# One transformer block on one core: the condition and beta fetched as one row each and spread by TensorE, one block of the modulation weights loaded and multiplied ahead of x

## The chip, the core and the metric

The kernel runs on one core of a Trainium2 chip. The metric is device time in microseconds (us) of one launch, and less is better. Three runs of the kernel before took 853.75, 854.21 and 854.20 us; their median is 854.2 us. Three abbreviations for engines come from the profile: PE is TensorE, DVE is VectorE, ACT is ScalarE; POOL is GpSimd and SP is SyncE, which issues most DMAs.

## The reference

The block takes x (2048 rows of 512), a condition row c (1x512) and weights, all in fp32. The change touches what is computed from c, from `beta` and from the first 1024 columns of `w_mod`:

```python
mod = (_silu(c) @ w_mod).reshape(c.shape[0], 6, 1, -1)
sa, ca, ga, sb, cb, gb = (mod[:, 0], mod[:, 1], mod[:, 2], mod[:, 3], mod[:, 4], mod[:, 5])
h = _layernorm(x, axis=-1) * (1 + ca) + sa
x = x + ga * _A_ref(h, A_wq, A_wk, A_wv, A_wo, A_beta)
h = _layernorm(x, axis=-1) * (1 + cb) + sb
x = x + gb * _B_ref(h, B_w_gate, B_w_up, B_w_down)
```

`_A_ref` is attention of 32 heads of width 16 over four segments of 512 rows, with a memory carried from segment to segment. `sigmoid(beta)`, one number a head, mixes memory and attention. `_B_ref` is a bilinear GLU of width 1376.

## The kernel before

The program is one long function, `tile_kernel`, that writes instructions out in order. It has three stages: a start, which ends with the projections of the first segment's first heads; attention with the rest of the projections woven in; and the GLU. PE's instructions are chained one behind the other in the order in which the code writes them (`MM`, `TP`), and `CV` and `CA` do the same for DVE and ACT in the start. So the order in the start is that of the code. DMAs issued by SP run in the order of SP's queue. Each DMA takes one of eight completion semaphores in turn (those of ACT's queue too), so an issue waits until the DMA eight places before it has landed.

All of the change lies in the start:

- ACT's queue fetches the condition as `s_c` (L628): the host has laid c out as 128 rows of 4 numbers, so 16 bytes go to each of 128 partitions. It then fetches `beta` to all 128 partitions as `be` (L669), 128 bytes each, all from the same source row.
- SP fetches x's first four tiles (`xload`, L643; 256 KB each), then the first half of the needed modulation weights (`wm0_load(0)`, L665): four blocks `wm0[k]`, 256 KB each, one for each group of 128 input rows. Behind these come `wk`'s first piece (L759), the second half (`wm0_load(1)`), `wq`'s first piece and four blocks of `wv`.
- PE runs 18 matmuls of zeros (`warm`, `wups`), each 128x512 in bf16, whose result nothing reads.
- ACT and DVE make silu(c) in `s_c` (L670 to L673): exp, plus one, reciprocal, product. GpSimd's four memsets of `kst` wait for the product.
- DVE takes the statistics of the four x tiles (`BATCH_NORM_STATS2`), ACT and DVE make 1/sd, and DVE normalises the tiles in place (`ln`, L203).
- PE computes the first half of sa and ca: `mod0(0)` (L719) multiplies four groups of 128 columns by silu(c), k = 0 to 3, with `s_c` repeated to 96 columns as the moving operand. A matmul in fp32 stands as two in the profile, so that is 32 passes. Then PE transposes the normalised x (`atp`, 16 transposes).
- For the second half, ACT scales block 0 by silu(c), DVE adds block 1 to that (`SCALAR_TENSOR_TENSOR`, L1112), and `mod0(1, (1, 2, 3))` needs 24 passes. Behind these stand the first projections `kps` and `qps`.

The call order at the start is this:

```python
lng = ln(pa, pa, xts.pop(0), 0, ca_c, sa_c, "a", ("h", 8, 2), True)
next(lng)                                        # statistics, 1/sd
mod0(0)
CA.activation(r0[1][0], r0[1][0], AF.Copy, scale=s_c[:, 0:1])
next(lng)                                        # normalise, transpose
mod0_out(0, mp0[0])
CV.scalar_tensor_tensor(r0[1][1], r0[1][1], s_c[:, 1:2], r0[1][0], op0=ALU.mult, op1=ALU.add)
mod0(1, (1, 2, 3))
```

## Time and profile before

| | |
|---|---|
| median of three runs | 854.2 us |
| the profiled execution's own time | 854.15 us |
| its span, first to last instruction | 852.4 us |
| PE busy | 835.3 us, 98% |
| DVE, ACT, POOL busy | 643.1, 499.0, 276.8 us |
| first matmul on real data begins | 8.79 us |
| first projection (`kps`) begins | 16.97 us |

Times in the views count from the span's start. A row of the timeline gives the start, the time from the first start to the last end of the merged instructions, the engine, the line, the operation with what it writes and reads, and in brackets how long the engine sat idle before it and what ended that. "SPq" and "ACTq" are the sequencers that issue DMAs; a DMA's duration there is the issue alone, and its time to landing stands in the view of DMA issues. A row of the view by windows gives for each stretch the busy time of each engine with the number of its instructions, the granted clock, the DMA engines' busy share and GB/s.

### The profile page before, as it was taken

How to read it: one execution, taken by the hardware profiler on the slowest of the kernel's cores; microseconds unless marked ns; L12 is line 12 of the kernel's file. 1: busy time of each engine (PE TensorE's matmuls, PEld its weight loads, DVE VectorE, ACT ScalarE, POOL GpSimd, SP SyncE). 2: the span in 40 equal slices, each digit the busy share in tenths (PEclk: the TensorE clock that was granted, in tenths of full speed). 3: DMA queues.
4: the chain of work that ended last, by engine and by line, in shares of the span. 5: the costliest groups of instructions: out<-in, count | busy, mean ns of one | idle time of the engine just before them, and what ended most of it. 6: DMA issues, size and time to landing. Idle time of an engine off the chain costs nothing.

```text
span 852.4 us, 14404 instructions
## 1 busy us (share of the span) xinstructions
PE 835.3 (98%) x4972; PEld 597.4 (70%) x4972; DVE 643.1 (75%) x1797; ACT 499.0 (59%) x760; POOL 276.8 (32%) x423
## 2 busy tenths in 40 slices
PE   9989999999999999999999999999999999999998
PEld 6756656666665656666665687888888778888886
DVE  7897768887778967787888359989987855447654
ACT  4758767787676876677545626344435555555330
POOL 2756627566565774675434610000000000000000
PEclk9999999999999999999999999999999999999999
DMA  9645435563545554466675466587650685335102
GB/s 271 155 152 155 121 104 141 158 179 115 143 106 166 144 165 106 122 170 213 195 216 155 145 192 230 189 287 271 253 201 28 234 271 210 121 135 184 43 8 98
DMA packets 83928, 139.57 MB, mean 164 GB/s; under 512 B 12720, under 2 KB 46768, under 8 KB 83856
## 3 DMA queue, kind: packets, MB, share of 16 engines
q1 hardware_dynamic: 83424, 138.51, 52.0%
q8 instruction: 39, 0.64, 0.3%
q14 instruction: 33, 0.27, 0.1%
q10 hardware_dynamic: 432, 0.15, 0.1%
HBM read 89.87 MB, written 48.50 MB: 162 GB/s over the span
## 4 chain that ended last, share of the span: by engine, by line
PE 61%; DVE 5%; ACT 1%; issue 0%; POOL 0%; DVEq 0%
PE acc L1358 14%; PE Xg L1289 7%; PE Xu L1289 6%; PE wops L85 5%; PE tb L85 5%; PE Yu L1289 4%; PE Yg L1289 4%; PE k L85 3%; PE q L85 3%; DVE q L39 2%; PE Zg L1289 1%; PE Zu L1289 1%; PE qps L85 1%; PE vps L85 1%; PE Xx L1289 1%; PE up L85 1%
## 5 line engine op out<-in xcount | busy, mean ns | idle before, releaser
L39 DVE CUSTOM_DVE_ANT_0 q<-q,cmask 128x384 f32<-128x384 f32 (+3 forms) x512 | 248.2, 503 | 71.1 <-PE q L85 63.5
L335 ACT ACTIVATE pt<-k 128x1024 f32<-128x1024 f32 x160 | 164.0, 1025 | 74.2 <-PE k L85 71.4
L341 POOL TENSOR_SCALAR_AFFINE_SELECT pt<-pt 128x256 f32<-128x256 f32 (+1 forms) x224 | 98.0, 452 | 137.2 <-ACT pt L335 136.9
L85 PE MATMUL q<-kst,qst 96*128 96x384 bf16 (+3 forms) x512 | 122.8, 302 | 6.5 <-DVE nm L39 5.1
L85 PE MATMUL k<-qst,kst 98*128 98x384 bf16 (+3 forms) x512 | 96.0, 299 | 1.6 <-ACT pt L335 1.3
L1366 DVE TENSOR_TENSOR xa<-xa,acc 128x512 f32<-128x512 f32 x95 | 64.9, 684 | 39.6 <-PE acc L1358 37.8
L85 PEld LDWEIGHTS <-qst 96*128 96x128 bf16 x512 | 43.9, 98 | 58.4 <-issue 43.6
L85 PE MATMUL tb<-pt,v 128*32 128x512 f32 (+3 forms) x1024 | 75.5, 436 | 0.0
L39 DVE DVE_READ_ACCUMULATOR2_ANT nm<- 128x1 f32 x512 | 71.8, 140 | 0.0
L85 PEld LDWEIGHTS <-kst 98*128 98x128 bf16 x512 | 44.4, 98 | 24.9 <-issue 8.8
L1358 PE MATMUL acc<-dH,mH 128*128 128x512 f32 (+1 forms) x152 | 60.3, 397 | 0.0
L1358 PE MATMUL acc<-dL,mH 128*128 128x512 f32 (+1 forms) x152 | 60.1, 395 | 0.0
L1358 PE MATMUL acc<-dH,mL 128*128 128x512 f32 (+1 forms) x152 | 60.0, 395 | 0.0
L85 PEld LDWEIGHTS tb<-pt,v 128*32 128x32 f32 x1024 | 28.7, 109 | 38.6 <-issue 35.7
L367 ACT ACTIVATE tsb<-tb 128x512 f32<-128x512 f32 x32 | 19.1, 596 | 31.6 <-PE tb L85 31.5
L1358 PEld LDWEIGHTS acc<-dH,mL 128*128 128x128 f32 (+1 forms) x152 | 28.5, 188 | 7.1 <-DVE mL L1309 0.3
L1358 PEld LDWEIGHTS acc<-dL,mH 128*128 128x128 f32 (+1 forms) x152 | 28.6, 188 | 7.0
L1358 PEld LDWEIGHTS acc<-dH,mH 128*128 128x128 f32 (+1 forms) x152 | 28.5, 188 | 6.8
L85 PE MATMUL kps<-ahH,wkH 128*128 128x512 f32 x64 | 29.4, 460 | 0.0
L85 PE MATMUL qps<-ahH,wqH 128*128 128x512 f32 x64 | 28.7, 448 | 0.2 <-DVE oL L39 0.2
L85 PE MATMUL vps<-wvH,ahH 128*128 128x512 f32 x64 | 28.3, 442 | 0.0
L85 PE MATMUL wops<-woH,oH 128*128 128x512 f32 x64 | 28.3, 442 | 0.0
(403 smaller groups left out, 2019.1 us busy)
## 6 DMA issues: line engine op xcount, KB each, us to landing
wm<-in_w_mod_dram SPq DMA_DIRECT2D x24, 256.0 KB, 3.9
kd<-k SPq DMA_DIRECT2D x16, 384.0 KB, 2.5
qd<-q SPq DMA_DIRECT2D x16, 384.0 KB, 3.5
kst<-kd SPq DMA_DIRECT2D x32, 192.0 KB, 3.2
qst<-qd SPq DMA_DIRECT2D x32, 192.0 KB, 3.7
x<-in_x_dram SPq DMA_DIRECT2D x16, 256.0 KB, 4.8
kst<-kd SPq DMA_DIRECT2D x32, 128.0 KB, 3.2
qst<-qd SPq DMA_DIRECT2D x32, 128.0 KB, 3.7
```

Source lines behind the costliest of these rows:

```text
L39: i = getattr(self.eng, name)(*a, **k)
L85: return pe(nc.tensor.matmul(*a, **k))
L335: ex = act.activation(pt, kp, AF.Exp, scale=0.25)
L341: sels[u, i] = nc.gpsimd.affine_select(w, w, pattern=[[0, w.shape[1]], [1, P]], compare_op=ALU.is_ge, fill=0.0, base=0, channel_multiplier=-1)
L367: act.activation(tsbs[u], tbs.pop(u), AF.Copy)
L1289: pe(nc.tensor.matmul(ps[0:n], a, b[:, k], start=first and c == 0, stop=last and c == 5, skip_group_check=True))
L1358: pe(nc.tensor.matmul(ps, a[0:m, t * P:(t + 1) * P], b[0:m], start=j == 0, stop=j == n - 1))
L1366: vec.tensor_add(xa, xa, ps)
```

## The change

The host passes c as one row. ACT's queue fetches it as one row of 512 numbers (`crow`), and beta as one row of 32 (`brow`). PE turns the condition into columns, by four matmuls of one contraction row each, and copies beta to all partitions by one more; both results stand in the second bank of `wups`. ACT and DVE read the condition there, and ACT copies beta into `be`. Of the first half of the modulation weights, block k = 0 is loaded ahead of x and multiplied ahead of the others. The 18 matmuls of zeros become nine: three at the start, two behind the spreading and four behind the product of block 0.

```diff
-    nc.scalar.dma_start(s_c, c)
+    crow = pa.tile([P, D], F32, tag="mem", name="crow", bufs=1)[0:1]
+    brow = pa.tile([P, D], F32, tag="pkr", name="brow", bufs=1)[0:1, 0:H]
+    nc.scalar.dma_start(crow, c)
+    nc.scalar.dma_start(brow, beta[None, :])
...
-    xts = {0: xload(0)}
-    NWU = 18
...
-    warm(NWU)
...
-    wm0_load(0)
+    wm0_load(0, (0,))
+    xts = {0: xload(0)}
...
+    warm(3)
+    cps = wups[:, 1, 0:KT]
+    for k in range(KT):
+        MM(cps[:, k:k + 1], crow[:, k * P:(k + 1) * P], ones[0:1, 0:1], start=k == 0, stop=k == KT - 1, skip_group_check=True)
+    bps = wups[:, 1, KT:KT + H]
+    MM(bps, ones[0:1, :], brow, start=True, stop=True, skip_group_check=True)
+    warm(2)
+    wm0_load(0, (1, 2, 3))
     r0 = [[a[:, j].rearrange("p i c -> p (i c)") for a in wm0] for j in range(2)]
-    nc.scalar.dma_start(be, beta[None, :].to_broadcast([P, H]))
-    act.activation(e1, s_c, AF.Exp, scale=-1.0)
-    CV.tensor_scalar_add(e1, e1, 1.0)
-    CV.reciprocal(e1, e1)
-    scl = CV.tensor_mul(s_c, s_c, e1)
+    act.activation(e1, cps, AF.Exp, scale=-1.0)
+    act.activation(be, bps, AF.Copy)
+    def condition():
+        CV.tensor_scalar_add(e1, e1, 1.0)
+        CV.reciprocal(e1, e1)
+        scl = CV.tensor_mul(s_c, cps, e1)
...
     lng = ln(pa, pa, xts.pop(0), 0, ca_c, sa_c, "a", ("h", 8, 2), True)
+    condition()
     next(lng)
-    mod0(0)
+    mod0(0, (0,))
+    warm(4)
+    mod0(0, (1, 2, 3))
```

In `mod0` the moving operand and the start flag are chosen by the half j and no longer by the list of blocks, which leaves the products what they were.

On PE, at the head of its queue, the program before has the 18 matmuls of zeros (two of their rows are shown), then the product of all four blocks (`m`, from `wm`), then the transposes of x:

```order
L85 LDWEIGHTS wu
L85 MATMUL wups<-wu 128x512
L85 MATMUL m_248<-s_c,wm_0_231 128x96 x4
L85 MATMUL m_248<-s_c,wm_1_232 128x96 x4
L85 MATMUL m_248<-s_c,wm_2_233 128x96 x4
L85 MATMUL m_248<-s_c,wm_3_234 128x96 x4
L88 MATMUL atp_0_318<-ident,x_0_202 128x128
```

In the changed program PE has this from the third matmul of zeros on, down to the second of the four that follow block 0:

```order
L85 MATMUL wups<-wu 128x512
L85 MATMUL wups<-ones,crow 128x1 x4
L85 MATMUL wups<-brow,ones 128x32
L85 LDWEIGHTS wu
L85 MATMUL wups<-wu 128x512
L85 LDWEIGHTS wu
L85 MATMUL wups<-wu 128x512
L85 MATMUL m_236<-s_c,wm_0_205 128x96 x4
L85 LDWEIGHTS wu
L85 MATMUL wups<-wu 128x512
L85 LDWEIGHTS wu
L85 MATMUL wups<-wu 128x512
```

So the spreading stands behind three matmuls of zeros, block 0 behind two more, and the other three blocks behind four more; from the transposes on, PE's order is the same in both programs.

SP's queue at its head, before:

```order
L643 DMA x_0_202<-in_x_dram 128x512
L643 DMA x_1_204<-in_x_dram 128x512
L643 DMA x_2_206<-in_x_dram 128x512
L643 DMA x_3_208<-in_x_dram 128x512
L665 DMA wm_0_231<-in_w_mod_dram 128x2x256
L665 DMA wm_1_232<-in_w_mod_dram 128x2x256
```

And in the changed program:

```order
L657 DMA wm_0_205<-in_w_mod_dram 128x2x256
L646 DMA x_0_210<-in_x_dram 128x512
L646 DMA x_1_212<-in_x_dram 128x512
L646 DMA x_2_214<-in_x_dram 128x512
L646 DMA x_3_216<-in_x_dram 128x512
L657 DMA wm_1_206<-in_w_mod_dram 128x2x256
```

One block of the weights has moved past the four tiles of x; what follows stands as before. DVE's order has not moved: the three steps of the condition still stand directly ahead of the first statistics of x. ACT has one instruction more, the copy of beta, behind the exp of the condition.

More of the change, by code (lines that the diff above doesn't have):

```diff
@@ L645, in xload, with wm0_load @@
         return xt
+    wm0 = []
+    for k in range(KT):
+        a = ap.tile([P, 2, 2, 256], F32, tag="pt", name=f"wm0_{k}", bufs=PT)
+        wm0.append(a)
+    def wm0_load(j, ks=range(KT)):
+        for k in ks:
+            pin(nc.sync.dma_start(wm0[k][:, j], wm[:, k, :].rearrange("p (i c) -> p i c", c=D)[:, 0:2, 256 * j:256 * j + 256]))
+    wm0_load(0, (0,))
     xts = {0: xload(0)}
-    NWU = 18
     wu = pa.tile([P, 512], BF, tag="rl", name="wu", bufs=1)
@@ L655, in warm @@
             MM(wups[:, 0], wu[:, 0:P], wu, start=True, stop=True)
-    warm(NWU)
-    wm0 = []
+    warm(3)
+    cps = wups[:, 1, 0:KT]
     for k in range(KT):
-        a = ap.tile([P, 2, 2, 256], F32, tag="pt", name=f"wm0_{k}", bufs=PT)
-        wm0.append(a)
-    def wm0_load(j):
-        for k in range(KT):
-            pin(nc.sync.dma_start(wm0[k][:, j], wm[:, k, :].rearrange("p (i c) -> p i c", c=D)[:, 0:2, 256 * j:256 * j + 256]))
-    wm0_load(0)
-    r0 = [[a[:, j].rearrange("p i c -> p (i c)") for a in wm0] for j in range(2)]
-    nc.scalar.dma_start(be, beta[None, :].to_broadcast([P, H]))
-    act.activation(e1, s_c, AF.Exp, scale=-1.0)
-    CV.tensor_scalar_add(e1, e1, 1.0)
-    CV.reciprocal(e1, e1)
-    scl = CV.tensor_mul(s_c, s_c, e1)
-    for a in kst:
-        tc.add_manual_dep(nc.gpsimd.memset(a[96:98].rearrange("p h t -> p (h t)").bitcast(F32), ONES2).ins, scl.ins.name, SYNC, reason="order")
+        MM(cps[:, k:k + 1], crow[:, k * P:(k + 1) * P], ones[0:1, 0:1], start=k == 0, stop=k == KT - 1, skip_group_check=True)
[3 more added lines that the diff above has]
+    wm0_load(0, (1, 2, 3))
+    r0 = [[a[:, j].rearrange("p i c -> p (i c)") for a in wm0] for j in range(2)]
+    act.activation(e1, cps, AF.Exp, scale=-1.0)
[4 more added lines that the diff above has]
+        scl = CV.tensor_mul(s_c, cps, e1)
+        for a in kst:
+            tc.add_manual_dep(nc.gpsimd.memset(a[96:98].rearrange("p h t -> p (h t)").bitcast(F32), ONES2).ins, scl.ins.name, SYNC, reason="order")
     def gates():
@@ L721, in mod0 @@
         for k in ks:
-            f = s_c[:, k:k + 1].to_broadcast([P, MW]) if len(ks) == KT or k > 1 else ones[:, 0:MW]
+            f = s_c[:, k:k + 1].to_broadcast([P, MW]) if j == 0 or k > 1 else ones[:, 0:MW]
             for i in range(4):
                 MM(ps[:, i], r0[j][k][:, i * P:(i + 1) * P], f,
-                   start=k == ks[0] and i == 0, stop=k == KT - 1, skip_group_check=True)
+                   start=k == j and i == 0, stop=k == KT - 1, skip_group_check=True)
     hcur = [None]
@@ L1669 @@
     vals[0] = vals[0].reshape(S, D)
-    vals[9] = vals[9].reshape(KT, P).T
+    vals[9] = vals[9].reshape(1, D)
     nc = _bacc.Bacc("TRN2", target_bir_lowering=False, num_devices=1, dynamic_dma_scratch_size=1024)
```

## Prediction

> **What bounds the kernel now.** I read the page first, then PE's waits, then the start in order of time, because the change ends at PE's instruction for the first transpose.

> ```profile
> span 852.4 us, 14404 instructions
> PE 835.3 (98%) x4972; PEld 597.4 (70%) x4972; DVE 643.1 (75%) x1797; ACT 499.0 (59%) x760; POOL 276.8 (32%) x423
> PE q L85 <- DVE nm L39: 5.1, 11, 1.0
> PE q L85 <- DMA qd<-q: 0.5, 1, 0.5
> DVE ast L39 <- DMA x<-in_x_dram: 1.0, 2, 0.5
> 17.00:38.00 21.00, 20.91 (x91) 16.38 (x91) 18.09 (x26) 17.36 (x28) 11.06 (x21) 1.00 0.77 178
> ```

> PE is busy 98% of the span. The next three rows are waits (total, times, longest): PE's greatest behind 17 us, its only one there for a DMA, and DVE's for x in the start. The last is a window: from 17 to 38 us PE is busy 20.91 of 21.00 us. PE, in program order, is the path, so the change is worth what it moves `kps`, the first projection, and the rest follows at the same distance. The start, in order of time:

> ```profile
> 0.82 1.81 SPq L643 DMA_DIRECT2D x<-in_x_dram  x4
> 1.69 6.82 PE L85 MATMUL wups<-wu 128*128 128x512 bf16 x18 [1.69 <-DVE wu L650]
> 2.67 2.38 SPq L665 DMA_DIRECT2D wm<-in_w_mod_dram  x4
> 3.70 0.20 ACT L670 ACTIVATE e<-s_c 128x4 f32<-128x4 f32 x1 [1.61 <-DMA s_c<-in_c_dram]
> 4.35 0.16 DVE L39 TENSOR_TENSOR s_c<-s_c,e 128x4 f32<-128x4 f32 x1
> 4.43 0.69 DVE L39 BATCH_NORM_STATS2 ast<-x 128x6 f32<-128x512 f32 x1
> 7.25 0.69 DVE L39 BATCH_NORM_STATS2 ast<-x 128x6 f32<-128x512 f32 x1 [0.50 <-DMA x<-in_x_dram]
> 8.07 0.66 DVE L39 BATCH_NORM_STATS2 ast<-x 128x6 f32<-128x512 f32 x1
> 8.77 0.18 DVE L39 BATCH_NORM_AGGREGATE amv<-ast 128x2 f32<-128x6 f32 x1
> 8.79 3.78 PE L85 MATMUL m<-s_c,wm 128*128 128x96 f32 x32 [0.27 <-DVE ast L39]
> 10.35 1.91 DVE L39 TENSOR_SCALAR x<-x,amv,ay 128x512 f32<-128x512 f32 x4
> 12.41 1.91 PE L88 MATMUL atp<-ident,x 128*128 128x128 f32 x16
> 12.58 0.72 ACT L39 ACTIVATE wm<-wm,s_c 128x512 f32<-128x512 f32 x1 [3.06 <-DMA wm<-in_w_mod_dram]
> 12.61 0.16 DVE L39 COPY modc<-m 128x2 f32<-128x2 f32 x1 [0.34 <-PE m L85]
> 12.68 0.15 DVE L39 TENSOR_SCALAR modc<-m 128x2 f32<-128x2 f32 x1
> 13.21 1.14 ACT L39 ACTIVATE wkH<-wrk 128x512 fp32r<-128x512 f32 x1
> 13.46 0.75 DVE L39 SCALAR_TENSOR_TENSOR wm<-wm,s_c,wm 128x512 f32<-128x512 f32 x1 [0.63 <-DMA wm<-in_w_mod_dram]
> 14.27 1.13 PE L85 MATMUL m<-ones,wm 128*128 128x96 f32 x8
> 15.24 1.95 PE L85 MATMUL m<-s_c,wm 128*128 128x96 f32 x16
> 16.97 0.48 PE L85 MATMUL kps<-ahH,wkH 128*128 128x512 f32 x1
> 26.84 1.84 POOL L765 TENSOR_TENSOR wkL<-wrk,wkH 128x512 fp32r<-128x512 f32 x1 [18.58 <-ACT wkH L39]
> ```

> From 8.79 us PE hardly rests: 32 passes to 12.41 (0.113 us each), 16 transposes, a wait of about 0.1 us for DVE's sum (done at 13.46 + 0.75 = 14.21), 24 passes to 16.97. What released the first pass was not DVE, as its bracket says, but a landing: the first `wm` issue (2.67) took 6.0 us to land, which is 8.67. These are the landing times, from the DMA views of the stretches 0.8 to 1.2 (two rows), 2.6 to 3.0, and 4.0 to 5.2 us:

> ```profile
> x<-in_x_dram SPq DMA_DIRECT2D x1, 256.0 KB, 2.7
> s_c<-in_c_dram ACTq DMA_DIRECT2D x1, 2.0 KB, 2.8
> wm<-in_w_mod_dram SPq DMA_DIRECT2D x1, 256.0 KB, 6.0
> wm<-in_w_mod_dram SPq DMA_DIRECT2D x2, 256.0 KB, 6.6
> ```

> Why does a block take 2.7 us at first and 6 later? The last two columns of the next rows are the DMA engines' busy share and GB/s; the last two rows are the queues between 3.5 and 5.5 us.

> ```profile
> 2.50:3.10 0.60, 0.60 (x3) 0.30 (x2) 0.27 (x2) 0.00 (x0) 0.00 (x0) 1.00 1.59 341
> 3.60:4.60 1.00, 1.00 (x3) 0.30 (x2) 0.59 (x4) 0.20 (x1) 0.00 (x0) 1.00 0.33 94
> 4.60:5.60 1.00, 1.00 (x4) 0.40 (x3) 0.70 (x2) 0.00 (x0) 0.96 (x2) 1.00 0.26 84
> 6.10:7.10 1.00, 1.00 (x4) 0.30 (x2) 0.62 (x2) 0.23 (x1) 1.00 (x2) 1.00 1.05 394
> q1 hardware_dynamic: 95, 0.16, 25.8%
> q10 hardware_dynamic: 103, 0.01, 3.7%
> ```

> The stream runs at 341 GB/s, falls to 94 and 84, and returns to 394. In the hole, 103 packets of q10 (ACT's queue) carry 0.01 MB: beta's 128 copies. Queue and hole coincide; that one causes the other is my inference. [...] The rows show a hole, but not its cause.

> **The change part by part.** The sum is made against the profiled execution: 854.15 us, of which 852.4 are span and 1.75 lie around it; the median shown is 854.2, 0.05 more.

> *Transfers.* At 390 GB/s the two slow seconds would have carried 390 + 390 KB; they carried 94 + 84. So 0.6 MB are missing, 1.55 us, and with the rest of the hole about 1.7. Without it x's last tile and the blocks behind it land up to 1.7 us earlier. The last first-half block (issued at 4.2, 6.6 to land, so 10.8) comes at 9.1; bounds 9.1 and 10.8. Block 0, now first in the queue, should land as x's first tile did, 2.7 us after an issue at 0.82: 3.5. Each x tile falls behind one more issue and one block, 0.45 to 0.7 us (2.38 / 4 an issue; 0.26 MB at 390 GB/s), to about 4.2 for the first. That costs nothing, because DVE is not yet there.

> *The condition.* Before, c lands at 3.65 and exp to product takes 3.70 to 4.51, 0.81 us. Now a row lands (2.9 to 3.65; I take 3.3, as the packets are fewer), and PE needs four matmuls, eight passes. No row shows a matmul of one contraction row; the nearest is 0.113 us a pass at full clock, and twice that at the clock of the start. So 0.9 to 1.8 us, I take 1.3, and 0.2 until the result is seen. With the 0.81 us, silu(c) stands at 5.6 (4.9 to 6.4), 1.1 later than before. This wait is new. Behind it on DVE stand the statistics of x. Before, they began at 4.43, but waited twice for x, 1.0 us in all; now x is there, and four at 0.82 us (7.25 to 8.07) and a last 0.88 give 5.65 + 2.46 + 0.88 = 9.0, against 8.95. So the normalisation ends at 12.3, as before. GpSimd's memsets behind silu(c) also start 1.1 later; its next work is at 26.8 us. ACT's copy of beta, 0.2 us, falls into its idle time.

> *The matmuls of zeros.* The 18 ended at 8.51, ahead of the landing at 8.67, so removing nine frees nothing. They did something else:

> ```profile
> L85 PE MATMUL wups<-wu x18: 379/634/634, 1.7 to 8.1; 128*128 128x512 bf16 x18
> 1.69:7.21 5.52, 5.52 (x13) 1.00 0.74 210
> L85 PEld LDWEIGHTS <-wu x18: 98/151/151, 1.7 to 7.9; 128*128 128x128 bf16 x18
> ```

> Thirteen took 5.52 us, 0.425 each, then one lasts 379 ns instead of 634: PE ran slow until 7.2 us. (The column of granted clock says 1.00 throughout, so here durations tell more.) All 32 passes before ran fast. How slow passes in fp32 are, no row shows; the weight load's 151 against 98 says at least 1.5 times, the matmuls' spacing about 2. I take 2, 0.225 us.

> *PE's new order.* Block 0's eight passes start with silu(c) at 5.6 and end at 7.4; the four zeros at 0.425 end at 9.1, and here they stand in the path, since blocks 1 and 2 have landed. If the clock has come by then, 24 passes at 0.113 end at 11.8, block 3 (9.1) being there. Transposes take 11.8 to 13.6, no longer behind 32 passes; DVE has the last x tile at 12.3. DVE's two copies and its sum, whose block no longer makes it wait, run from 12.3 to 13.4. So the 24 passes of the second half start at 13.6 instead of 14.27: **0.6 us earlier**, after the 0.05 or so that PE waits at the hand-over. Behind that ACT has scaled its block and split `wk`, 1.9 us of work that starts with a landing 1.7 earlier, so `kps` follows.

> *When does the clock come?* Before, 5.5 us after the first matmul. If the broken stretch from 1.7 us counts, 7.2; if only the unbroken one from 5.6, 11.1. Up to 9.1 the gain stays 0.6; behind that every us costs half a us, so at 11.1 it is 0.6 - 1.0 = -0.4. I take 9.2, the middle. [...]

> Sum: 854.15 - 0.6 = 853.55, and with the 0.05 to the median **853.6 us**.

> **Rivals.**

> *The hole stays* (it has another cause, or the rows go in many tiny pieces). For it: only coincidence speaks for beta. Against: the stream is whole before and after. Then block 3 lands at 10.8 and the first half ends at 11.7, so the transposes still end by 13.5; but DVE's sum waits for its block as before, to 14.21, and the second half starts at 14.27. Gain 0: 854.2.

> *The clock comes late* (slower). The place is PE between 9.1 and the transposes. If neither the short matmuls nor the passes in fp32 count as busy enough, the clock waits for the transposes or later; for it: no row before shows passes at the slow clock being followed by a faster one, only dense bf16 did that. Against: the nine zeros and the passes leave few gaps. It decides from about 10.3 us on, where the gain is 0. At 15.6 us: 24 passes at 0.225 from 9.1 to 14.5, five slow transposes to 15.6, eleven fast to 16.8, second half 16.8 instead of 14.27: 2.5 us slower, 856.7.

> *All goes early.* The row lands at 2.9, its passes take 0.9, silu(c) stands at 4.9, the clock comes by 7.5. Block 0 4.9 to 6.7, zeros to 7.9, blocks 1 to 3 behind the landing at 9.1 to 10.6; transposes to 12.4; DVE's sum ends at 12.7, as the statistics then begin 0.7 earlier. Second half at 12.75: 1.5 us earlier, and up to 0.5 more if PE's one wait for a DMA behind 17 us goes as well: 852.2 to 852.7, say 852.5.

> **How the numbers follow.** The forecast, gain -0.4 to 1.3 with 0.6 likeliest, gets 0.62 (852.9 to 854.6). The hole stays: 0.14. Clock late: 0.11. All early: 0.13. A measurement of this kernel can tell about 0.2%, 1.7 us, from no change. The clock's rival is slower by more (856.7): 0.10 of its 0.11, and a little for what I have not seen: 0.11 in all. All early straddles the bound, 1.5 to 2.0; I count it beyond, for the earlier transfers may also help behind 17 us: 0.13. The rest, 0.76, lies within. The range takes in both ends of the unknown costs and part of the clock's rival: 852.4 to 855.2.

> **What would show it right or wrong.** Right: no stretch under 200 GB/s between 3 and 6 us; `crow` landing near 3.3; silu(c) near 5.6 and statistics dense behind it; the 24 passes of the first half at 0.113 us from about 9.1; transposes starting at 11.8, `kps` near 16.4, and everything behind 17 us at one distance. Wrong: passes at 0.2 us beyond 11 us; DVE's sum still waiting for its block at 13.4; silu(c) beyond 6.4; or a shift at `kps` that is not that of the end.

## The result, and the profile after

The changed kernel takes **856.27 us** (median of seven runs, 855.37 to 856.76) against 854.2 us for the kernel before on the same chip (seven runs, 852.63 to 855.03). The ratio is 1.0024, with a 95% interval of 1.0014 to 1.0034: slower by 2.1 us, where 853.6 was forecast and 855.2 was the upper end of the range. The execution profiled after took 856.27 us, its span is 854.6.

Of two kernels below, `own_psum` and `sixteen`, one execution each, the profiled one, is left out of all figures, because PE ran slow in it from the first instruction to the last (1381.84 and 2129.46 us); their traces are not used.

The first two lines of the page of after: PE is busy 98% as before, with 1.4 us more, and DVE and ACT with a little less.

```profile
span 854.6 us, 14404 instructions
PE 836.7 (98%) x4973; PEld 600.5 (70%) x4973; DVE 642.5 (75%) x1797; ACT 498.8 (58%) x761; POOL 275.8 (32%) x423
```

The start of after in order of time:

```profile
3.08 1.86 PE L85 MATMUL wups<-ones,crow 1*128 1x1 f32 x8
4.81 0.61 PE L85 MATMUL wups<-brow,ones 1*128 1x32 f32 x2
5.35 1.03 PE L85 MATMUL wups<-wu 128*128 128x512 bf16 x2
6.42 0.17 ACT L678 ACTIVATE e<-wups 128x4 f32<-128x4 f32 x1 [4.33 <-PE wups L85]
7.15 0.16 DVE L39 TENSOR_TENSOR s_c<-wups,e 128x4 f32<-128x4 f32 x1
7.23 0.68 DVE L39 BATCH_NORM_STATS2 ast<-x 128x6 f32<-128x512 f32 x1
7.36 2.02 PE L85 MATMUL m<-s_c,wm 128*128 128x96 f32 x8 [0.98 <-DVE s_c L39]
9.18 1.91 PE L85 MATMUL wups<-wu 128*128 128x512 bf16 x4
10.88 4.14 PE L85 MATMUL m<-s_c,wm 128*128 128x96 f32 x24
11.91 1.91 DVE L39 TENSOR_SCALAR x<-x,amv,ay 128x512 f32<-128x512 f32 x4
14.86 1.91 PE L88 MATMUL atp<-ident,x 128*128 128x128 f32 x16
15.06 0.16 DVE L39 COPY modc<-m 128x2 f32<-128x2 f32 x1 [1.24 <-PE m L85]
15.20 0.74 DVE L39 SCALAR_TENSOR_TENSOR wm<-wm,s_c,wm 128x512 f32<-128x512 f32 x1
16.60 1.03 PE L85 MATMUL m<-ones,wm 128*128 128x96 f32 x8
19.20 0.48 PE L85 MATMUL kps<-ahH,wkH 128*128 128x512 f32 x1
```

Three places carry the result. The condition's columns are done at 3.08 + 1.86 = 4.94, but exp begins only at 6.42: it waits for PE. PE then stands for 0.98 us ahead of block 0. And 24 passes take 4.14 us where the sum had 2.7, so the transposes begin at 14.86. DVE, done with x at 13.82, waits 1.24 us for PE. `kps` starts at 19.20 instead of 16.97, 2.23 us late, and the span ends 2.2 later.

The view by windows; the first three stretches are those shown before the change, and the last two show PE's clock:

```profile
3.60:4.60 1.00, 1.00 (x7) 1.00 (x6) 0.00 (x0) 0.00 (x0) 0.00 (x0) 1.00 1.08 275
4.60:5.60 1.00, 1.00 (x5) 0.81 (x6) 0.00 (x0) 0.00 (x0) 0.00 (x0) 1.00 0.65 221
6.10:7.10 1.00, 0.28 (x1) 0.00 (x0) 0.35 (x2) 0.49 (x3) 0.00 (x0) 1.00 1.02 345
11.89:13.59 1.70, 1.70 (x10) 1.70 (x9) 1.68 (x4) 1.41 (x2) 0.00 (x0) 1.00 1.13 331
13.59:15.29 1.70, 1.70 (x17) 1.70 (x16) 0.46 (x4) 0.00 (x0) 0.00 (x0) 1.00 1.05 373
```

The hole is gone (275 and 221 GB/s, before 94 and 84); what is left of it is half a microsecond at 127 GB/s, from 4.5 to 5.0 us. Between 11.89 and 13.59 us PE touches 10 matmuls in 1.7 us, behind that 17 in the same time: the clock came in between. The trace's own record of the clock has its first entry at full rate at 13.64 us (before: 7.32). As in the profile before, the column of granted clock reads 1.00 until that record begins; the counts tell more.

### The profile page after: what moved, and what is told of

It reads as the page before. It is cut to its first block, busy times and chain, and to the rows that moved or that the text cites. A ratio compares the mean times of both kernels' runs of the same rounds, so it can differ in the third digit from the quotient of the medians.

```text
span 854.6 us, 14404 instructions
## 1 busy us (share of the span) xinstructions
PE 836.7 (98%) x4973; PEld 600.5 (70%) x4973; DVE 642.5 (75%) x1797; ACT 498.8 (58%) x761; POOL 275.8 (32%) x423
## 4 chain that ended last, share of the span: by engine, by line
PE 60%; DVE 4%; ACT 2%; POOL 2%; issue 1%; DMA 0%; DVEq 0%; ACTq 0%; POOLq 0%
PE acc L1373 14%; PE Xu L1304 7%; PE Xg L1304 7%; PE wops L85 5%; PE tb L85 4%; PE Yu L1304 4%; PE Yg L1304 4%; PE k L85 3%; PE q L85 3%; DVE q L39 2%; PE Zg L1304 1%; PE Zu L1304 1%; PE qps L85 1%; PE vps L85 1%; PE ctp L88 1%; ACT pt L335 1%
## 5 line engine op out<-in xcount | busy, mean ns | idle before, releaser
L39 DVE CUSTOM_DVE_ANT_0 q<-q,cmask 128x384 f32<-128x384 f32 (+3 forms) x512 | 248.2, 503 | 72.3 <-PE q L85 64.6
L85 PE MATMUL q<-kst,qst 96*128 96x384 bf16 (+3 forms) x512 | 122.8, 302 | 6.4 <-DVE nm L39 5.3
L85 PE MATMUL k<-qst,kst 98*128 98x384 bf16 (+3 forms) x512 | 95.9, 299 | 1.6 <-ACT pt L335 1.3
L85 PEld LDWEIGHTS <-qst 96*128 96x128 bf16 x512 | 43.9, 98 | 57.8 <-issue 42.5
L85 PE MATMUL tb<-pt,v 128*32 128x512 f32 (+3 forms) x1024 | 75.8, 436 | 0.3 <-POOL pt L341 0.3
L39 DVE DVE_READ_ACCUMULATOR2_ANT nm<- 128x1 f32 x512 | 72.0, 141 | 0.0
L85 PEld LDWEIGHTS <-kst 98*128 98x128 bf16 x512 | 44.5, 98 | 25.0 <-issue 9.0
L85 PEld LDWEIGHTS tb<-pt,v 128*32 128x32 f32 x1024 | 28.6, 109 | 39.1 <-issue 35.5
L85 PE MATMUL kps<-ahH,wkH 128*128 128x512 f32 x64 | 29.4, 460 | 0.0
L85 PE MATMUL qps<-ahH,wqH 128*128 128x512 f32 x64 | 28.7, 448 | 0.0
L85 PE MATMUL wops<-woH,oH 128*128 128x512 f32 x64 | 28.3, 442 | 0.1
L85 PE MATMUL vps<-wvH,ahH 128*128 128x512 f32 x64 | 28.3, 442 | 0.0
## 6 DMA issues: line engine op xcount, KB each, us to landing
wm<-in_w_mod_dram SPq DMA_DIRECT2D x24, 256.0 KB, 4.0
x<-in_x_dram SPq DMA_DIRECT2D x16, 256.0 KB, 4.4
```

The source lines that it names most:

```text
L39: i = getattr(self.eng, name)(*a, **k)
L85: return pe(nc.tensor.matmul(*a, **k))
```

## The experiments

All ratios are against the kernel before, run on the same chip in the same batch. They are worked out from the single executions and are not the quotients of the medians beside them.

| kernel | what it is | median, us | before, us | ratio, 95% interval |
|---|---|---|---|---|
| after | the whole change | 856.27 | 854.2 | 1.0024 (1.0014 to 1.0034) |
| own_bank | after, spread in a PSUM tile of its own | 854.75 | 853.83 | 1.0010 (0.9989 to 1.0030) |
| beta_copies | after, beta fetched as before | 855.74 | 853.83 | 1.0034 (1.0013 to 1.0056) |
| beta_row | before, beta as one row | 853.77 | 853.83 | 0.9999 (0.9991 to 1.0008) |
| block_first | before, block 0 ahead | 853.85 | 853.83 | 1.0001 (0.9992 to 1.0011) |
| act_plus_one | before, one ACT instruction more | 853.81 | 853.62 | 1.0004 (0.9995 to 1.0013) |
| beta_psum | beta_row, read in PSUM | 853.25 | 853.62 | 0.9997 (0.9988 to 1.0006) |
| zeros_nine | before, 9 matmuls of zeros | 856.32 | 853.62 | 1.0029 (1.0017 to 1.0041) |
| own_psum | own_bank, beta read in PSUM | 853.71 | 853.62 | 1.0000 (0.9991 to 1.0009) |
| sixteen | beta_psum, 16 zeros | 852.76 | 853.46 | 0.9989 (0.9980 to 0.9998) |
| zeros_twenty | before, 20 zeros | 854.10 | 853.46 | 1.0005 (0.9996 to 1.0014) |
| both_parts | sixteen, block 0 ahead | 852.84 | 853.46 | 0.9988 (0.9979 to 0.9996) |
| own_seven | own_psum, 7 zeros | 853.35 | 853.46 | 0.9998 (0.9989 to 1.0006) |

**own_bank: does exp wait for the zeros?** Exp and the zeros write and read the same PSUM tile, `wups`. Here the spread condition and beta get a tile of their own.

```diff
-    cps = wups[:, 1, 0:KT]
+    spread = pst((P, 512), "sm", "spread")
+    cps = spread[:, 0:KT]
...
-    bps = wups[:, 1, KT:KT + H]
+    bps = spread[:, KT:KT + H]
```

> The changed kernel with the spread condition and beta in a PSUM bank of their own and not beside the result of the matmuls of zeros; nothing else differs. Theory 1 (two causes: ACT's exp waits for the two zeros behind the spreading since it shares a tile with them, and PE's clock comes late): exp starts near 5.5 instead of 6.42 us, silu(c) stands near 6.35 instead of 7.31, the x statistics begin as much earlier, and kps comes 0.5 us earlier (clock still at 13.6) to 2.2 us earlier (clock by 9.8): 854.1 to 855.8 us. Theory 2 (the clock alone is the cause): exp moves, but kps moves by less than 0.5 us: 855.8 to 856.4. Theory 3 (exp waits for the short matmuls themselves, not for the zeros): exp stays at 6.4, time stays 856.3.

Measured: 854.75 us, with an interval that includes both no change and the ratio of after. The start of own_bank in order of time:

```profile
5.46 0.17 ACT L679 ACTIVATE e<-spread 128x4 f32<-128x4 f32 x1 [3.36 <-PE spread L85]
6.18 0.16 DVE L39 TENSOR_TENSOR s_c<-spread,e 128x4 f32<-128x4 f32 x1
6.40 2.02 PE L85 MATMUL m<-s_c,wm 128*128 128x96 f32 x8
9.70 2.81 PE L85 MATMUL m<-s_c,wm 128*128 128x96 f32 x24
16.69 0.48 PE L85 MATMUL kps<-ahH,wkH 128*128 128x512 f32 x1
```

Exp is 0.96 us earlier, about the two zeros' time, and starts just behind beta's passes (4.81 + 0.61), which still share its tile. Block 0 has no idle time ahead of it, and the 24 passes take 2.81 us instead of 4.14: in this execution the clock came at 9.45 us. `kps` stands at 16.69, 0.28 earlier than before the change and 2.51 earlier than in after. This execution, at 853.64 us, is one of the two fastest of eleven, so most of the others gained less. The wait of exp is shown: it comes from a tile shared with matmuls that exp has nothing to do with.

**beta_copies: is the hole beta's?** After, with c as a row but beta fetched to 128 partitions as before.

```diff
-    nc.scalar.dma_start(brow, beta[None, :])
+    nc.scalar.dma_start(be, beta[None, :].to_broadcast([P, H]))
...
-    bps = wups[:, 1, KT:KT + H]
-    MM(bps, ones[0:1, :], brow, start=True, stop=True, skip_group_check=True)
...
-    act.activation(be, bps, AF.Copy)
```

> The changed kernel, but beta goes to 128 partitions by DMA as before and is not spread by PE; the condition stays a row. Theory 1 (beta's 128 copies make the hole in the DMA stream): the stream falls under 150 GB/s for 2 us or more between 3 and 6.5 us, and the blocks behind x land 1.5 to 2 us later than in the changed kernel; since PE is late there anyway the time moves by less than 0.7 us (855.6 to 857). Rival (the hole had another cause, such as the condition's 16-byte pieces or the first x tiles): no stretch of 1 us under 200 GB/s between 3 and 6 us, landings as in the changed kernel.

The windows of beta_copies:

```profile
3.60:4.60 1.00, 1.00 (x7) 1.00 (x6) 0.00 (x0) 0.00 (x0) 0.00 (x0) 1.00 0.76 101
4.60:5.60 1.00, 1.00 (x4) 0.38 (x4) 0.00 (x0) 0.00 (x0) 0.00 (x0) 1.00 0.42 106
```

The hole is back, 101 and 106 GB/s; with beta as a row in the kernel before (beta_row, next) the same stretches are full:

```profile
3.60:4.60 1.00, 1.00 (x3) 0.30 (x2) 0.67 (x4) 0.21 (x1) 0.04 (x1) 1.00 0.97 334
4.60:5.60 1.00, 1.00 (x4) 0.40 (x3) 0.97 (x3) 0.00 (x0) 1.00 (x2) 1.00 0.96 331
```

The 128 copies make the hole, whichever way c comes. How they do it stays open: their own packets take only a few per cent of the DMA engines' time (3.7% in the prediction's row of q10). The time, 855.74 us, is not clean: the profiled execution took 861.46 us by an accident at 34 us that the last section tells of.

**beta_row and block_first: the parts alone, on the kernel before.** beta_row fetches one row and spreads it behind the first half's product:

```diff
-    nc.scalar.dma_start(be, beta[None, :].to_broadcast([P, H]))
+    nc.scalar.dma_start(brow, beta[None, :])
...
     mod0(0)
+    bps = wups[:, 1, 0:H]
+    MM(bps, ones[0:1, :], brow, start=True, stop=True, skip_group_check=True)
+    act.activation(be, bps, AF.Copy)
```

> The kernel before with one part of the change: beta fetched as one row and spread by one matmul, which stands behind the first half's product; condition, order of loads and the 18 zeros as before. Theory 1 (beta's copies make the hole; the zeros and PE's order decide what it is worth): no hole, the first w_mod block lands near 7.0 instead of 8.7 us, but the zeros hold PE until 8.5, so kps moves by 0 to 0.4 us earlier: 853.8 to 854.2 us. Rival (the hole is not beta's): landing stays at 8.7, time 854.2 to 854.5.

block_first loads and multiplies block 0 ahead of x, behind all 18 zeros, with c and beta as before:

```diff
+    wm0_load(0, (0,))
     xts = {0: xload(0)}
...
-    wm0_load(0)
+    wm0_load(0, (1, 2, 3))
...
-    mod0(0)
+    mod0(0, (0,))
+    mod0(0, (1, 2, 3))
```

> The kernel before with one part of the change: the first w_mod block loaded ahead of x and multiplied ahead of the others; condition, beta and the 18 zeros as before (the hole in the stream too). Theory 1 (order alone is worth nothing, since the later blocks and the second half land as before): first passes at 8.5, the last block lands at 10.8 and the transposes end by 14.1, second half at 14.2 to 14.3: 854.0 to 854.6 us. Rival (the order itself costs, by x that lands later and statistics that end later): normalisation ends 0.7 us or more later, kps 0.3 to 0.8 us later: 854.6 to 855.2.

Neither moves the time (0.9999 and 1.0001). So the loss of the whole change is to be looked for in the third part, the way of the condition with its broken zeros. In beta_row's profile `kps` starts at 15.83, 1.14 us earlier than before and not the 0 to 0.4 expected: in this execution the clock came at 5.49 us (before: 7.32), and so the zeros ended 0.9 us sooner. Yet the span is only 0.1 shorter: PE loses 1.0 us at 366 to 373 us, where POOL waits 1.81 us for the last block of `wo` (0.54 before). That needed an answer of its own, below.

**zeros_nine: what do the zeros do?** The kernel before with half of them.

```diff
-    NWU = 18
+    NWU = 9
```

> The kernel before with nine matmuls of zeros instead of 18, and nothing else. Theory (the zeros decide when the clock comes): they end at 5.5 us or so, PE stands until the first block lands at 8.7, the stretch is broken, the 32 passes start at the slow clock at 0.2135 us each and the full clock comes between 12 and 16 us; kps 1.5 to 3 us later: 855.3 to 857. Rival (removing nine frees nothing and costs nothing, as the prediction had it of their end): 853.8 to 854.2.

It costs 2.7 us (1.0029, 1.0017 to 1.0041), more than the whole change. The windows of zeros_nine:

```profile
5.09:6.79 1.70, 0.17 (x1) 0.00 (x0) 0.95 (x3) 0.21 (x1) 1.70 (x3) 1.00 0.72 266
6.79:8.49 1.70, 0.00 (x0) 0.00 (x0) 1.26 (x4) 0.02 (x1) 1.43 (x2) 0.88 1.08 383
8.49:10.19 1.70, 1.37 (x7) 1.40 (x7) 0.98 (x5) 0.50 (x2) 0.00 (x0) 0.50 1.11 346
13.59:15.29 1.70, 1.70 (x11) 1.70 (x11) 0.00 (x0) 0.78 (x1) 0.00 (x0) 0.61 1.12 329
```

Here the granted clock shows it openly, since it had been granted once: PE idles from 5.26 to 8.82, the column falls to 0.50, and only from 14.91 us on is it full again. The same kernel in order of time; all 32 passes run slow:

```profile
8.82 6.69 PE L85 MATMUL m<-s_c,wm 128*128 128x96 f32 x32 [3.56 <-DVE ast L39]
19.69 0.48 PE L85 MATMUL kps<-ahH,wkH 128*128 128x512 f32 x1
```

6.69 us for 32 passes (before: 3.78), and `kps` 2.72 us late. So the 18 zeros, which end at 8.51 us, left the clock full for the passes that begin at 8.79 in the kernel before; nine, which end at 5.26, did not. Their result is read in neither, so what made the difference is how long they last.

**act_plus_one and beta_psum: where did beta_row's microsecond go?** In the profiles that lost it, a packet of 16 KB on the queue of instructions (q8) fell 1.1 to 1.4 us behind the issue of the last `wo` block, inside its transfer; in the others 2.2 us or more behind it. First theory: ACT's instructions, since those kernels have one more of them. act_plus_one adds one to the kernel before; beta_psum takes beta_row's away, as the gates read beta in PSUM.

```diff
     act.activation(e1, s_c, AF.Exp, scale=-1.0)
+    act.activation(gg[:, 0:1], epst, AF.Copy)
```

> The kernel before with one ScalarE instruction more, a copy of one column behind silu's exp that nobody reads (its tile is written in full later). Theory (ACT's instruction fetch): from then on ACT has executed one instruction more at each point of the program, its fetch of 16 KB comes about 1 us earlier against the transfer of the last wo block, that block takes about 3.7 us instead of 2.7, and PE loses about 1.0 us at 366 to 373 us: about 854.8 against 853.8 of the kernel before. Rival (the wo block is late because everything ahead of it is early): nothing changes, wo takes 2.7 us, 853.8.

```diff
     def gates():
+        be = wups[:, 1, 0:H]
...
-    act.activation(be, bps, AF.Copy)
```

> beta as one row as in beta_row, but the gates read it in PSUM, so ACT's copy falls away and ACT has as many instructions as in the kernel before. Theory (ACT's instruction fetch): wo's last block takes 2.7 us again, and the 1.1 us that kps is early, as in beta_row, are kept to the end: 852.7 to 852.9. Rival (early work always runs into wo's block): wo 3.7 to 3.9 us, the gain is lost at 366 us as in beta_row: 853.8.

The theory fell, both ways: act_plus_one's packet came at 2.19 us and the block in 2.6, beta_psum's at 1.16 us, and POOL waited 1.7. What the losers share is one or two matmuls more on PE ahead of that place. The page of the profile has 39 packets on q8 for 4972 matmuls, 127 to a packet with as many weight loads, so they look like PE's instruction fetch; that they are is an inference from this count.

**zeros_twenty and sixteen: the same from PE's side.** Two matmuls more than before, and beta_psum with two fewer, which gives PE as many as before.

```diff
-    NWU = 18
+    NWU = 20
```

> The kernel before with 20 matmuls of zeros instead of 18, and nothing else: two matmuls and loads more on PE, 0.4 us of them behind the first block's landing. Theory (PE's instruction fetch): the fetch comes 1.1 to 1.5 us after wo's last issue, inside its transfer, wo takes 3.6 to 3.9 us, PE loses 1.0 us at 366 to 373 us beside the 0.2 to 0.4 at the start: 854.8 to 855.2. Rival (the fetch has nothing to do with it): 853.8 to 854.2, wo 2.7 us.

```diff
-    NWU = 18
+    NWU = 16
```

> beta_psum with 16 matmuls of zeros instead of 18, so that PE has as many instructions before the last wo block as in the kernel before (two of zeros less, beta's two passes more). Theory (PE's instruction fetch, 16 KB per 127 matmuls and their weight loads): the fetch falls 2.2 us after wo's last issue again, behind its transfer, wo takes 2.5 to 2.8 us, POOL waits about 0.5 us for it, and the lead at kps is kept at 366 us; 852.4 to 853.0. Rival (early work always runs into wo's block): POOL waits 1.7 to 1.8 us, 853.3 to 853.8.

The DMA view of zeros_twenty, from 0.8 to 2.0 us behind the last `wo` issue (packets, MB, share of 16 engines):

```profile
q8 instruction: 1, 0.02, 5.0%
```

And from its view of the tile `wor`, the wait ahead of POOL's product (us, times):

```profile
  DMA wor<-in_wo_dram: 1.5, 1
```

The packet lies inside the transfer, 5.0% of 16 engines for 1.2 us, that is one engine for 0.96 us. POOL waits 1.5 us (before 0.5), and PE goes from 0.34 us early to 0.38 late between 366 and 373 us. So the trace shows the packet, the wait and a loss on PE of 0.7 us. At the start nothing was lost, where 0.2 to 0.4 us were expected (`kps` at 16.96, before 16.97). The median is 0.64 us above that of the kernel before, where 1.0 to 1.4 were expected, and the interval includes no change, so the time by itself proves nothing. Why one or two matmuls move the packet by about a microsecond is not shown. `sixteen` is faster (0.9989, 0.9980 to 0.9998), as expected, but has no usable trace; that its gain was kept at 366 us is argued, not shown.

**own_psum and own_seven: the changed kernel, mended.** own_psum reads beta in PSUM, in the zeros' tile, so that exp's tile holds the condition alone; own_seven also takes two of the four zeros behind block 0 away.

```diff
-    bps = spread[:, KT:KT + H]
+    bps = wups[:, 1, 0:H]
...
-    act.activation(be, bps, AF.Copy)
```

> own_bank (the changed kernel with the spread condition in a PSUM tile of its own), with beta read by the gates in PSUM and no copy by ACT. Theory (ACT's instruction fetch): wo's last block takes 2.7 us, PE keeps the 1.0 us at 366 us that own_bank loses, and the time is about 1 us below own_bank: 853.5 to 853.9. Rival (the fetch has nothing to do with it): 854.7 as own_bank.

```diff
     mod0(0, (0,))
-    warm(4)
+    warm(2)
     mod0(0, (1, 2, 3))
```

> The changed kernel mended in three places: the spread condition in a PSUM tile of its own, beta read in PSUM without ACT's copy, and two of the four zeros between block 0 and the other blocks left out (seven in all). Theory (exp's wait was 1 us, the clock sets the rest): silu(c) at 6.3, passes of block 0 at 6.4, the other 24 from 9.3 at the earliest; where the clock comes by 9.8 kps is at 16.3 and the time 852.8 to 853.4, where it comes at 13.2 up to 1.7 us more, so a median of 853.0 to 854.5 with a spread of about 1.7 us. Rival (the zeros taken out are what the clock needs): the clock comes at 13 us or later in most executions, 855 to 856.

Both are level with the kernel before, 1.0000 and 0.9998, and their intervals end below the point where that of after begins. own_psum came out at the figure of the theory that has fallen by now; a likelier reason is in own_seven, at the start in order of time:

```profile
4.81 0.61 PE L85 MATMUL wups<-brow,ones 1*128 1x32 f32 x2
4.98 0.17 ACT L679 ACTIVATE e<-spread 128x4 f32<-128x4 f32 x1 [2.89 <-PE spread L85]
5.68 0.16 DVE L39 TENSOR_TENSOR s_c<-spread,e 128x4 f32<-128x4 f32 x1
6.18 1.86 PE L85 MATMUL m<-s_c,wm 128*128 128x96 f32 x8
8.68 4.16 PE L85 MATMUL m<-s_c,wm 128*128 128x96 f32 x24
17.03 0.47 PE L85 MATMUL kps<-ahH,wkH 128*128 128x512 f32 x1
```

With a tile that nothing else writes, exp starts 0.04 us behind the columns, 1.44 us earlier than in after, and silu(c) stands at 5.84. PE has no gap. Still the passes are slow: the clock came at 11.50 us here, at 9.45 in own_bank. The 24 passes take 4.16 us, as in after (4.14). So the 2.17 us by which `kps` is ahead of after are not the clock's: 1.18 come from block 0's earlier start (6.18 against 7.36) and 1.02 from the shorter way from there to the 24 passes, with two zeros less (2.50 against 3.52). own_seven's eleven runs spread over 3.1 us (852.05 to 855.19), both_parts' over 1.7.

**both_parts: what is left when the condition goes the old way.** sixteen with block 0 ahead: no hole, 16 zeros in one piece. The diff is against the kernel before; beta's DMA and the gates are as in sixteen and not shown again.

```diff
+    wm0_load(0, (0,))
     xts = {0: xload(0)}
...
-    NWU = 18
+    NWU = 16
...
-    mod0(0)
+    mod0(0, (0,))
+    mod0(0, (1, 2, 3))
+    bps = wups[:, 1, 0:H]
+    MM(bps, ones[0:1, :], brow, start=True, stop=True, skip_group_check=True)
```

> sixteen with the changed kernel's order of loads as well: block 0 ahead of x, its eight passes ahead of the other three blocks'; c comes as 128x4 as before, 16 zeros without a break. Theory (what cost time was the way of c and the broken stretch of zeros, the block ahead is harmless and helps where PE waits for it): no gap of 1 us ahead of the first pass, clock by 8.5 us, kps 15.6 to 16.2; 852.2 to 853.0. Rival (block ahead delays x, and x's normalisation sets the transposes): kps 16.3 to 16.9 as in block_first; 853.3 to 853.9.

It beats the kernel before and after: 852.84 us, 0.9988 of the kernel before (0.9979 to 0.9996), 0.6 us less. Against sixteen (852.76 us, 0.9989) it gains nothing that the times show. So they credit what the two share, beta's row read in PSUM and 16 zeros, and not block 0's place. Its start:

```profile
1.69 5.12 PE L85 MATMUL wups<-wu 128*128 128x512 bf16 x16 [1.69 <-DVE wu L650]
6.65 1.03 PE L85 MATMUL m<-s_c,wm 128*128 128x96 f32 x8
8.21 2.92 PE L85 MATMUL m<-s_c,wm 128*128 128x96 f32 x24 [0.54 <-DMA wm<-in_w_mod_dram]
15.80 0.48 PE L85 MATMUL kps<-ahH,wkH 128*128 128x512 f32 x1
```

The clock is there at 4.75 us, block 0 fills a place where PE would wait, `kps` is 1.17 us early, and POOL's wait for `wo` is 0.4 us. The lead is kept to the end in this execution (span 850.6 against 852.4).

## Why the prediction was wrong, point by point

**Transfers: right.** The prediction took the hole for beta's copies and called that an inference; beta_copies and beta_row show it. Block 0 landed 2.9 us behind its issue at 0.82, at 3.7 (3.5 forecast); the last of the first half, issued near 4.2, took 5.3 us, to 9.5 (9.1). From 3.6 to 4.6 us the stream ran at 101 GB/s with the copies (beta_copies) and at 334 without them (beta_row); how they slow it is not shown.

**The condition: the step that failed first.** The forecast had silu(c) at 5.6: the row at 3.3, spreading 1.3, "0.2 until the result is seen", 0.81 for the rest. Measured: 3.08, 1.86, 1.48 and 0.89, which makes 7.31. The row was 0.22 early and spreading 0.56 long, just beyond its bound of 1.8; but the 0.2 was 1.48. The prediction asked what PE does ahead of exp and not what shares exp's tile: beta's two passes and two zeros stand behind the columns, in the same PSUM tile, and exp waited for them all. Given a tile of its own, in own_seven, silu(c) stands at 5.84, within the bounds.

**The zeros: half right.** "Removing nine frees nothing" holds for their end. That taking them away could cost something was seen, but weighed too lightly: in zeros_nine it costs 2.7 us.

**The clock: the second step that failed.** The likeliest value was 9.2 us, the middle between a stretch counted from 1.7 and one counted from 5.6; it came at 13.64. Since block 0 began at 7.36 with a gap ahead of it, even the pessimistic count, 5.5 us of unbroken work, gives 12.9. And the 5.5 is the figure of one execution: counted from the first zeros at 1.69, which ran without a break, the clock came after 3.0 us in zeros_nine (4.67), 3.1 in both_parts (4.75), 3.8 in beta_row (5.49) and, by the same record, 5.6 in the kernel before (7.32). What sets the moment is not shown. In zeros_nine the clock fell 3.42 us after it came, a stretch in which PE was busy 0.6 us.

What held the clock back in after is not shown either. The gap of 0.98 us may have a part in it. In zeros_nine and beta_copies the changes of the clock lie multiples of 3.41 us apart (see the last section). If such steps also reach back from the first change, which no run shows, the step before the last ends at 10.23 in after, and PE was busy in 2.87 us of it. But in beta_psum the clock came at 4.50, behind 2.81 us of zeros alone in its step (1.09 to 4.50), and in own_seven a step without any gap did not bring it (4.67 to 8.08). Counted so, the gap alone does not decide.

**The sum.** The second half began at 16.60 and not at 13.6. Of the 3.0 us, block 0's later start is 1.76 (7.36 against 5.6). Its passes and four zeros took 3.52 us, as forecast (3.5). The 24 passes took 3.98 up to the transposes, not 2.7, which is 1.28: the clock. So the late condition cost more than the late clock. Slow passes were sized rightly, 0.225 forecast, 6.69 / 32 = 0.209 measured.

**DVE's side: right, and without effect.** The normalisation ended at 13.82, 1.5 us later than forecast for the 1.7 that silu(c) was late; PE was later still.

**The rivals.** "The clock comes late" is what happened, at a chance of 0.11. Its condition, later than 10.3 us, held. Its price of 2.5 us was near the 2.1 measured by luck, for it was worked out with block 0 at 5.6 and the clock at 15.6, not at 7.36 and 13.64. Of its reason, that neither the short matmuls nor the passes in fp32 count, the second half is refuted: in own_bank passes and zeros brought the clock at 9.45. The first half may hold, as the last section tells. With exp's wait gone the loss went too, in own_psum and own_seven, although own_seven's clock was still late. How much each mend brings is not separated by the times, since own_bank, with the first alone, has too wide an interval. "The hole stays" is refuted by the windows of after. "All goes early" needed silu(c) at 4.9; what such a start is worth shows in both_parts, where it stands at 4.54 and the clock came at 4.75: 1.17 us at `kps`, not 1.5.

**The signs.** Of those named as right, the row's landing came, and the statistics stood dense behind silu(c). The hole's end came but for the half microsecond at 127 GB/s, which is under the 200 named. The fast passes from 9.1, the transposes at 11.8 and `kps` at 16.4 did not come. Of those named as wrong, two came together: silu(c) beyond 6.4, and slow passes beyond 11 us.

**What follows behind 17 us.** "The rest follows at the same distance" held within a microsecond: 2.23 us at `kps`, up to 3.1 between, 2.2 at the end. It isn't exact: in after a packet of q8, by its count PE's instruction fetch, came 1.35 us behind the issue of the last `wo` block and not 2.26 as before, the block took 3.8 us to land instead of 2.7, and PE lost 0.9 us there; it won some back later. One more instruction on ACT cost nothing that the times show, as forecast for the copy of beta (act_plus_one, 1.0004, 0.9995 to 1.0013).

## What to carry to other kernels

Before a small result is put into a tile that is at hand, look at who else writes that tile ahead of the reader: in after exp began 1.48 us behind the columns that it reads, in own_seven, with a tile of its own, 0.04. The number of matmuls of zeros ahead of real work decided whether PE's clock was full for it in the kernel before and in zeros_nine: 3.78 us for 32 passes behind 18 of them, 6.69 behind nine. So ask of a new order when the clock will come, and not only whether the zeros end in time. Whether a gap ahead of the clock delays it is not shown. One behind it, 1.03 us in block_first, left the 24 passes that followed fast (2.92 us), while in one of 3.56 us in zeros_nine the granted clock fell to 0.50. Here a late operand and a late clock together cost 2.1 us. The broadcast of 128 bytes to 128 partitions on a second queue went with 94 and 84 GB/s in the kernel before and with 101 and 106 in beta_copies. One row with one small matmul left 334 and 331 (beta_row), and the matmul, which stands behind the first half's product there, cost nothing that the times show (0.9999).

## What the runs showed of the hardware

- **One-row matmuls seem not to bring the clock.** In own_seven PE was busy without a gap from 1.69 us on; the clock still came only at 11.50. Its windows:

```profile
5.09:6.79 1.70, 1.70 (x8) 1.22 (x7) 1.42 (x6) 0.06 (x1) 0.82 (x1) 1.00 0.93 334
6.79:8.49 1.70, 1.70 (x8) 1.19 (x8) 1.63 (x5) 0.00 (x0) 1.70 (x3) 1.00 1.05 358
8.49:10.19 1.70, 1.70 (x9) 1.70 (x9) 1.00 (x5) 0.50 (x2) 1.10 (x2) 1.00 1.11 337
10.19:11.89 1.70, 1.70 (x11) 1.70 (x11) 1.63 (x6) 0.27 (x1) 0.00 (x0) 1.00 1.10 348
11.89:13.59 1.70, 1.70 (x18) 1.70 (x18) 1.17 (x5) 1.50 (x2) 0.00 (x0) 1.00 1.12 330
```

- **A packet on q8, by its count an instruction fetch, seems to hold up a transfer.** In zeros_twenty one packet of 16 KB holds one DMA engine for 0.96 us, and the 256 KB block that it falls into lands in 3.6 us. In the kernel before, which has two matmuls of zeros less at its start, the packet comes 2.26 us behind the issue of that block, at 363.09, and the block lands in 2.7.

- **DVE seems to be shut out by POOL.** In beta_copies one instruction of DVE took 8.87 us. Its row, in order of time:

```profile
34.52 8.87 DVE L861 SCALAR_TENSOR_TENSOR phk<-phk,rlk 128x512 f32<-128x512 f32 x1 [1.03 <-ACT phk L856]
```

The same instruction took 3.80 us in the kernel before; others of its kind take 0.70 (median):

```profile
33.57 3.80 DVE L853 SCALAR_TENSOR_TENSOR phk<-phk,rlk 128x512 f32<-128x512 f32 x1 [1.02 <-ACT phk L848]
```

  POOL ran additions and products of two tiles without a pause from 34.48 to 42.85 us, and DVE's instruction ended 0.5 us behind them. That POOL's work held it up is inferred from this, not tried by itself. PE was busy 0.86 us between 38.00 and 41.40, and its clock fell at 41.46 and came back at 48.28. Windows of beta_copies:

```profile
38.00:41.40 3.40, 0.86 (x4) 0.30 (x3) 3.40 (x1) 1.80 (x3) 3.40 (x6) 1.00 0.95 224
41.50:44.90 3.40, 0.78 (x3) 0.61 (x3) 3.37 (x6) 0.00 (x0) 1.35 (x2) 0.50 0.65 192
44.90:48.20 3.30, 3.30 (x10) 2.14 (x10) 1.16 (x5) 0.00 (x0) 0.00 (x0) 0.50 0.76 279
```

  PE is behind by 0.9 us ahead of this place and by 7.9 behind it. Of the runs of its batch, two of ten of beta_copies (861.46 and 863.21), one of own_bank (861.65) and one of the kernel before (860.08) lie 5.7 us or more above their medians; that all four have this cause is a guess, and it was seen in one only.
